# The first layer from its fourth tile on by quadrants with seven products for eight, its left sides streamed from DRAM

## Chip, cores and metric

One core of one Trainium2 chip. The metric is the time of one execution of the program on the device in microseconds (us); lower is better. Times are medians of several runs; stages are read from one execution recorded by the hardware profiler.

## What is computed

An attention with pooled keys and values (pooled by 8), and two dense layers of 512 to 2048 to 512 behind it, all in float32:

```python
scores = scale * np.matmul(q, k_p.transpose(0, 1, 3, 2))       # batch 8, 8 heads, 576 positions, 72 pooled keys
attn = np.exp(scores - np.max(scores, axis=-1, keepdims=True))
attn = attn / (np.sum(attn, axis=-1, keepdims=True) + 1e-09)
x = np.matmul(attn, v_p)                                       # to 4608 tokens x 512
h = x @ moe_w_in;  x = np.maximum(0.01 * h, h) @ moe_w_out     # first layer
h = x @ moe2_w_in; x = (h * np.clip(h + 3.0, 0.0, 6.0) / 6.0) @ moe2_w_out   # second layer
```

## The kernel before

Matrix products run in TensorE's float32r form. To keep the precision of float32 each operand is split in two parts, high and low, and each product is three matmuls: high x high, high x low, low x high.

**First layer.** The 4608 tokens are nine tiles of 512: tile b holds 512 of the 576 positions of batch b, and the ninth the 64 positions that are left of each of the eight batches. `moe_tile` takes one tile through 16 steps, one for each 128 columns of the hidden layer: `gemm1` (12 matmuls, lines 663 to 665), the leaky activation on ScalarE (line 678), the split of the result in `split_g` (a copy on ScalarE, line 286, and a subtraction on VectorE, line 296), and `gemm2` (12 matmuls, lines 712 to 714), which adds up in four banks of PSUM, y0 to y3. So a tile is 384 matmuls with 512 columns each. The sixteen weights w0 to w15 stay in SBUF, split, for all tiles; `decode_w` makes them from packed input words in the first two tiles. Tiles 0 and 1 are begun while batch 0 and 1 come out of the attention, in halves of 288 and 224 columns; tile 0 has a second part (weights 9 to 15) after tile 1.

**Attention.** Each batch is four units (`attend`): scores on TensorE, maxima on VectorE, exponentials on ScalarE (line 476), normalising on VectorE (line 508), transposes (lines 526, 544) and the product with the values (line 571) on TensorE. The units of batch t+1 are put among the steps of tile t, at `Jobs` slots (a tile has 34, one before each gemm1 and each gemm2).

**Second layer.** It goes by pairs of token groups (`Pair`), five pairs of 2 x 460 or 2 x 462 columns. The 2 x 2 quadrants of the weights and of the tokens are combined so that seven block products do for eight, in both products (`first` and `second`). A pair is 672 matmuls (line 911). The combined right sides are made by VectorE (`sides`, `second_sides`, line 818) and split; the combined left sides are made by `quadrant_weights` during tiles 2 to 8, stored to DRAM as w1s and w2s, and streamed back for every pair in transfers of 1 MB into four buffers (`stream`: raw twice, xh, xl).

**What sets the order.** All work is recorded as tasks, with an engine, a cost and the buffers that they read and write. `Plan.order` lays them out by repeated list scheduling with the costs and due times, forward and back, and the program is written in that order; each engine then works in its order. A buffer's tag with `bufs=n` rotates over n places in the order of the recording. All DMAs are issued by SyncE in one queue (SP), which waits at its head for what the next DMA needs. Where TensorE would wait in the beginning, `order` puts in fillers (`idle<-zeros`) up to `plan.fill_until`, the third step of tile 0.

Of the kernel before, what the change touches and what calls it, by code (L numbers as in the profile page):

```python
# [22 lines left out]
NF = DFF // 128  # L23
# [22 lines left out]
    slow=[0, 5, 5, 5, 5],  # L46
)
# [184 lines left out]
def attention_moe_moe(ctx: ExitStack, tc: tile.TileContext, qt, kt, vm, vr, wt, wq, eye, mask, out):  # L232
# [7 lines left out]

    nc = tc.nc
# [11 lines left out]
    def f32(ap):  # L253
        return ap.bitcast(F32)
# [58 lines left out]
    class Unit:  # L313


        def __init__(self, b, g, h):
            self.b, self.g, self.h = b, g, h
            self.fresh = h == 0
            self.early = b == 0 and h == 0
            self.whole32 = None  # L320
# [115 lines left out]
    def scores(u):  # L436

        assert held_keys[u.g] == u.b
        s = buf("s", [128, 1024], F32, 2)
# [114 lines left out]
    def values(u, x, spill):  # L554
# [19 lines left out]
        for pi, ps in enumerate(pss):  # L574
            k = 2 * u.g + pi

            if u.h == 0:
                dst = x((0, k), lambda t, k=k: t[:, k, 0:HALF])
                copy(dst, ps(None, lambda t: t[:, 0:HALF]), HALF, True, 0.125)
            else:  # L580
                n = TOK - HALF
                dst = x((1, k), lambda t, k=k: t[:, k, HALF:TOK])
# [5 lines left out]
    w = {}  # L588

# [5 lines left out]
    def decode(raw, t, l):  # L595

        words = lambda: raw.get().bitcast(I32).rearrange("p (n two) -> p n two", two=2)
        bits = lambda v: v.ap().bitcast(I32)

        on_act(1024, lambda: ACT.mul(out=t.ap(), in_=f32(words()[:, :, 1]), mul=2.0**-112), [raw()], [t])  # L600

        on_act(
            1024, lambda: ACT.mul(out=bits(l), in_=words()[:, :, 0].bitcast(U32), mul=7.49 / 2**32), [raw()], [l]
        )
        on_dve(
            1024,
# [7 lines left out]
            1024,  # L614
# [7 lines left out]
    def decode_w(f, raw, t, l):  # L622
# [7 lines left out]
        subtract(lo, t, hi, 1024)  # L630

# [11 lines left out]
    def split_x(x32, x, half=None):  # L643
        c0, c1 = (0, TOK) if half is None else HALVES[half]
        for k in range(4):
            cut = lambda t, k=k: four(t)[:, k, c0:c1]
            key = None if half is None else (half, k)
# [5 lines left out]
    def gemm1(f, x, c0, c1):  # L653
# [14 lines left out]
        keys = [(h, k) for h in part for k in range(4)]  # L668
# [89 lines left out]

    x2 = [buf(f"x2_{t}", [128, 4, TOK], pool=dram) for t in range(NT)]
    xr = buf("xr", [128, 4, B * REST], pool=dram)  # L760

    def store_y(ys, dst, r, last=False, plus=False):

        for o in range(4):
            v = r(("y", o), lambda t, o=o: four(t)[:, o, :])
# [11 lines left out]
            if o % 2 or last:  # L777
# [4 lines left out]
                    lambda o0=o0, o=o, d=d: DMA.dma_start(out=d(), in_=four(r.get())[:, o0 : o + 1, :]),  # L782
# [31 lines left out]
    w1s = [buf(f"w1s{j}", [128, PRODUCTS, 2, 512], F32R, pool=dram) for j in range(NF // 4)]  # L814
    w2s = [[buf(f"w2s{s}{h}", [128, 4, 512], F32R, pool=dram) for h in range(2)] for s in range(PRODUCTS)]
# [13 lines left out]
    def quadrant_weights(f):  # L829


        t = []
        for i in range(2):
# [7 lines left out]
            t.append(buf("s", [128, 1024], F32, 2))  # L841
            decode(raw, t[i](), buf("st", [128, 1024], F32, 3)())
        q = [[t[i](j, lambda t, j=j: t[:, 512 * j : 512 * j + 512]) for j in range(2)] for i in range(2)]

        def split_off(v, s):
            st = new_st(F32R)
            src = View(v.buf, v.key, lambda t: v.cut(t).rearrange("p (g n) -> p g n", g=2))
            hi, lo = [st(i, lambda t, i=i: t[:, :, 256 * i : 256 * i + 256]) for i in range(2)]
            copy(hi, src, 512)
            subtract(lo, src, hi, 512)  # L850
            for g, (dst, cut) in enumerate(
                [
                    (w1s[f // 2], lambda t: t[:, s, f % 2, :]),
                    (w2s[s][f // 4], lambda t: t[:, f % 4, :]),
                ]
            ):
                dst = dst((s, f), cut)
                on_dma(
                    262144,
                    lambda dst=dst, g=g: DMA.dma_start(out=f32(dst.ap()), in_=f32(st.get()[:, g, :])),  # L860
                    [st()],
                    [dst],
                )

        (q11, q12), (q21, q22) = q
        split_off(q11, 0)
        split_off(q12, 1)
        split_off(q22, 5)
        plus(q22, q21, q22, 512)
        split_off(q22, 4)  # L870
        minus(q21, q11, q21, 512)
        split_off(q21, 3)
# [549 lines left out]
```

## Time and profile before

| | |
|---|---|
| median of 3 runs | 1652.26 us (1652.09 to 1656.89) |
| the profiled execution: own time, span in the profile | 1655.2 us, 1652.9 us |
| matmuls of the built program, fillers among them | 7939, 201 |
| TensorE busy | 1639.3 us, 99% of the span |
| VectorE busy | 980.3 us, 59% |
| ScalarE busy | 894.7 us, 54% |
| DMA | 276.24 MB, 167 GB/s in the mean |

The profiled execution's own time is 2.94 us above the median of the runs. A matmul's recorded duration (390 ns) is longer than the distance between two of them, since they are pipelined; what a stage costs TensorE is read from how many there are in a stretch. The same holds for VectorE and ScalarE: of two instructions back to back, the distance between their starts counts.

### The profile page before, as it was taken

What the parts mean: (1) busy time and instruction counts of PE and PEld (TensorE: products, weight loads), DVE (VectorE), ACT (ScalarE), POOL (GpSimd) and SP (SyncE); (2) the same over time, 40 slices, a digit from 0 to 9 for tenths busy, and PEclk for the clock granted to TensorE, in tenths of its full rate; (3) what the DMA queues carried; (4) which work ended last, traced back from release to release, by engine and by line L of the source; (5) the groups of instructions that cost most, each with busy time, mean ns of one, the idle gap of its engine ahead of it and who ended that gap; (6) DMA issues with size and microseconds to landing.
All of it is one profiled execution on the core that took longest, in us unless ns stands there. A gap on an engine that the chain in (4) does not pass through costs nothing.

```text
span 1652.9 us, 22384 instructions
## 1 busy us (share of the span) xinstructions
PE 1639.3 (99%) x8169; PEld 1413.1 (85%) x8169; DVE 980.3 (59%) x1748; ACT 894.7 (54%) x2233; POOL 2.8 (0%) x14
## 2 busy tenths in 40 slices
PE   8999999999999999999999999999999999999999
PEld 8888888888888888888888898888889888888988
DVE  7996245545355454457421458846856875695584
ACT  7985355455554655556432345545555554564454
POOL 0000000000000000000000000000000000000000
PEclk9999999999999999999999999999999999999999
DMA  7642043323233231346610266776676586567564
GB/s 261 237 171 88 8 141 123 118 98 115 86 109 121 95 135 69 117 148 220 204 49 1 99 236 220 247 252 218 230 268 215 205 286 224 212 244 238 204 224 153
DMA packets 76925, 276.24 MB, mean 167 GB/s; under 512 B 13712, under 2 KB 26128, under 8 KB 55568
## 3 DMA queue, kind: packets, MB, share of 16 engines
q1 hardware_dynamic: 76816, 274.82, 47.7%
q8 instruction: 64, 1.05, 0.3%
q14 instruction: 45, 0.37, 0.1%
HBM read 223.41 MB, written 51.38 MB: 166 GB/s over the span
## 4 chain that ended last, share of the span: by engine, by line
PE 91%; DVE 5%; ACT 2%; DMA 1%; issue 1%; SPq 0%; DVEq 0%; ACTq 0%
PE y L911 17%; PE a L911 12%; PE h L911 11%; PE y L712 8%; PE y L713 8%; PE y L714 7%; PE h L663 7%; PE h L664 7%; PE h L665 7%; PE a L451 2%; PE a L571 2%; ACT s L476 1%; PE a L526 1%; DVE raw L354 1%; DMA raw<-kt 1%
## 5 line engine op out<-in xcount | busy, mean ns | idle before, releaser
L712 PE MATMUL y<-gh,w 128*128 128x512 f32 (+2 forms) x604 | 237.9, 394 | 0.0
L296 DVE TENSOR_TENSOR gl<-u,gh 128x512 fp32r<-128x512 f32 (+2 forms) x151 | 100.1, 663 | 231.7 <-ACT gh L286 231.4
L663 PE MATMUL h<-xh,w 128*128 128x512 f32 (+2 forms) x604 | 235.3, 390 | 1.3 <-ACT u L678 1.3
L713 PE MATMUL y<-gl,w 128*128 128x512 f32 (+2 forms) x604 | 232.5, 385 | 0.0
L714 PE MATMUL y<-gh,w 128*128 128x512 f32 (+2 forms) x604 | 231.6, 383 | 0.0
L664 PE MATMUL h<-xl,w 128*128 128x512 f32 (+2 forms) x604 | 230.7, 382 | 0.0
L665 PE MATMUL h<-xh,w 128*128 128x512 f32 (+2 forms) x604 | 230.6, 382 | 0.0
L678 ACT ACTIVATE u<-h 128x512 f32<-128x512 f32 (+2 forms) x151 | 87.9, 582 | 148.3 <-PE h L665 136.7
L286 ACT CAST gh<-u 128x512 fp32r<-128x512 f32 (+2 forms) x147 | 89.3, 608 | 133.6 <-PE y L714 108.3
L476 ACT ACTIVATE s<-a,mx 96x72 f32<-96x72 f32 x384 | 115.8, 325 | 39.4 <-DVE mx L470 39.4
L714 PEld LDWEIGHTS y<-gh,w 128*128 128x128 f32 x604 | 113.6, 188 | 24.6
L665 PEld LDWEIGHTS h<-xh,w 128*128 128x128 f32 x604 | 113.5, 188 | 23.5
L663 PEld LDWEIGHTS h<-xh,w 128*128 128x128 f32 x604 | 113.5, 188 | 23.4 <-ACT u L678 1.5
L664 PEld LDWEIGHTS h<-xl,w 128*128 128x128 f32 x604 | 113.6, 188 | 21.7
L712 PEld LDWEIGHTS y<-gh,w 128*128 128x128 f32 x604 | 113.7, 188 | 21.1
L713 PEld LDWEIGHTS y<-gl,w 128*128 128x128 f32 x604 | 113.8, 188 | 20.8 <-DVE gl L296 0.3
L289 ACT ACTIVATE gh<-w 128x460 fp32r<-128x460 f32 (+1 forms) x140 | 81.9, 588 | 66.9 <-PE y L911 37.3
L289 ACT ACTIVATE s<-w 128x460 fp32r<-128x460 f32 (+1 forms) x140 | 82.4, 589 | 64.8 <-PE y L911 33.5
L1089 DVE SCALAR_TENSOR_TENSOR s<-w,s 128x460 fp32r<-128x460 f32 (+1 forms) x140 | 88.7, 633 | 29.6 <-ACT s L289 29.5
L1089 DVE SCALAR_TENSOR_TENSOR gl<-w,gh 128x460 fp32r<-128x460 f32 (+1 forms) x140 | 88.2, 633 | 24.5 <-ACT gh L289 24.4
L911 PE MATMUL y<-w,raw 128*128 128x460 f32 (+1 forms) x384 | 86.3, 369 | 0.0
L476 ACT ACTIVATION_READ_ACCUMULATOR s<-a,mx 96x1 f32 x384 | 81.5, 212 | 0.0
(209 smaller groups left out, 3046.9 us busy)
## 6 DMA issues: line engine op xcount, KB each, us to landing
raw<-w2s SPq DMA_DIRECT2D x36, 1024.0 KB, 4.8
raw<-w1s SPq DMA_DIRECT2D x32, 1024.0 KB, 5.0
xh<-w1s SPq DMA_DIRECT2D x20, 1024.0 KB, 4.9
xh<-w2s SPq DMA_DIRECT2D x17, 1024.0 KB, 4.8
xl<-w2s SPq DMA_DIRECT2D x17, 1024.0 KB, 4.8
raw<-wq SPq DMA_DIRECT2D x16, 1024.0 KB, 5.0
w<-wt SPq DMA_DIRECT2D x15, 1024.0 KB, 7.3
w1s<-st SPq DMA_DIRECT2D x56, 256.0 KB, 2.2
```

What stands on the lines that cost most here:

```text
L286: a = lambda: ACT.copy(out=dst.ap(), in_=src.ap())
L289: a = lambda: ACT.mul(out=dst.ap(), in_=src.ap(), mul=scale)
L296: lambda: DVE.tensor_tensor(out=dst.ap(), in0=a.ap(), in1=f32(b.ap()), op=ALU.subtract),
L476: ACT.activation(out=at()[:, c, h, :], in_=s4()[:, c, e, :], func=AF.Exp, scale=1.0 / 64.0, bias=mx.get()[:, c, h : h + 1], accum_out=sm.g ...
L663: PE.matmul(out=o, lhsT=hi, rhs=xh.get()[:, k, c0:c1], start=k == 0, stop=False)
L664: PE.matmul(out=o, lhsT=hi, rhs=xl.get()[:, k, c0:c1], start=False, stop=False)
L665: PE.matmul(out=o, lhsT=lo, rhs=xh.get()[:, k, c0:c1], start=False, stop=k == 3)
L712: PE.matmul(out=y[:, n0:n1], lhsT=hi, rhs=gh.get()[:, n0:n1], start=start, stop=False)
L713: PE.matmul(out=y[:, c0:c1], lhsT=hi, rhs=gl.get()[:, c0:c1], start=False, stop=False)
L714: PE.matmul(out=y[:, c0:c1], lhsT=lo, rhs=gh.get()[:, c0:c1], start=False, stop=stop)
L911: PE.matmul(out=o, lhsT=l, rhs=r, start=first and i == m == 0, stop=last and i == len(left) - 1 and m == 2, skip_group_check=True,)
L1089: lambda: DVE.scalar_tensor_tensor(out=lo.ap(), in0=v.ap(), scalar=1.0 / 6.0, in1=f32(hi.ap()), op0=ALU.mult, op1=ALU.subtract),
```

## The change

Tiles 0, 1 and 2 stay as they were. The first layer's tiles 3 to 8 become three pairs of tiles, (3, 4), (5, 6) and (8, 7), each worked like a pair of the second layer, with 2 x 512 columns (`Pair1`, a subclass of `Pair`). What comes with it:

- Left sides of the first layer. `keep` (called by `decode_w`) stores each decoded weight to DRAM (chunk, 0.5 MB) and stores three quadrants of 0.25 MB of its split form directly (left1). `first_weights` reads chunks back, and makes the other four combinations (`combine`, `split_off`: 4 differences or sums, 4 copies, 4 subtractions), at slots of tiles 1, 0 (second part) and 2.
- Left sides of the second layer. `second_weights` does what `quadrant_weights` did, in halves of 512 columns: f = 0 and 1 in tile 1, f = 2 in the first pair, 3 and 4 in the second, 5 to 7 in the third.
- Streams of the new pairs come in pieces of 0.5 MB into six places, the halves of xh, xl and w15 (`rows = 2`).
- Attention. Batches 3 and 4 are done in tile 2 (eight units, three slots apart), 5 and 6 in the first pair, 7 in the second. A batch that must wait for its pair goes to DRAM (x1) and back.
- The exponentials' buffers are s and sb, one place each, in place of s with two. The results of tile 2 leave by st.

The diff, cut to its core:

```diff
@@ decode_w
     copy(hi, t, 1024)
     subtract(lo, t, hi, 1024)
+    keep(f, t, wf)
+
+def keep(f, t, wf):
+    d = chunk[f]()
+    on_dma(1 << 19, lambda: DMA.dma_start(out=d.ap(), in_=t.ap()), [t], [d])
+    r, lower = f % 8, f >= 8
+    for g, sides in enumerate(([(5, 1)], [(1, 0), (5, 1)]) if lower else ([(0, 0), (1, 1)], [(0, 0)])):
+        for s, h in sides:
...
...
+                    lambda dst=dst, g=g, h=h: DMA.dma_start(
...
+                        in_=f32(wf.get()[:, g : 4 : 2, 256 * h : 256 * h + 256]),
@@ left sides
+def combine(left, f, q):
+    (q11, q12), (q21, q22) = q
+    plus(q22, q21, q22, 512)
+    split_off(left, f, q22, 4)
+    minus(q21, q11, q21, 512)
+    split_off(left, f, q21, 3)
+    minus(q11, q22, q11, 512)
+    split_off(left, f, q11, 2)
+    minus(q12, q12, q11, 512)
+    split_off(left, f, q12, 6)
+def first_weights(f):
+    t = new_raw()
...
+    combine(left1[0], f, quarters(t))
+def second_weights(f):
...
+        for j in range(2):
+            decode(raw, q[i][j], new_st()(None, lambda t: t[:, 0, :]), j)
...
+    combine(left2, f, q)
@@ Pair.side (the right sides), for both layers
+        def side(self, s, b, split):
+            (b11, b12), (b21, b22) = b
+            if s == 2:
+                t2 = self.tmp()
+                minus(b11, b12, b11, n)
+                minus(t2, b22, b11, n)
+                minus(b21, b21, t2, n)
+                split(t2)
+            else:
+                if s == 3:
+                    minus(b12, b22, b12, n)
+                split({0: b11, 1: b21, 3: b12, 4: b11, 5: b21, 6: b22}[s])
@@ Pair1
+    class Pair1(Pair):
+        left = left1[0]
+        banks = {
+            "x": [("h", 2), ("h", 2), ("y0", 1), ("y1", 1)],
+            "z": [("y2", 1), ("y3", 1)],
+            "w": [("y0", 1), ("y1", 1), ("h", 2), ("h", 2)],
+        }
+        rows = 2
+        split_in = ["g", "sb", "g"]
+        def new_spare(self):
+            t, u = new_st(), buf("u", [128, 512])
+            self.spare = [u(), *(t(i, lambda t, i=i: t[:, i, :]) for i in range(2))]
+        def stream_to(self):
+            if not self.pieces:
+                for tag in ("xh", "xl", "w15"):
+                    t = buf(tag, [128, 4, 512], F32R)
+                    self.pieces.extend(t(i, lambda t, i=i: t[:, 2 * i : 2 * i + 2]) for i in range(2))
+            return lambda n: take("piece", self.pieces)
+        def activate(self, dst, h, in_psum):
+            leaky(dst, h, self.n, in_psum)
+        def place_of(self, i, j):
+            to = x2[self.tiles[j]]
@@ the main program
-    for t in range(2, NT):
-        jobs = Jobs()
...
-            attend_all(jobs, range(4 * t + 4, 4 * t + 8), (0, 8, 16, 24), held, SLOW)
-            jobs.at(14, lambda t=t: quadrant_weights(t - 2))
...
-        ys = moe_tile(x, jobs, FULL)
+    pairs1 = [Pair1(3, 4), Pair1(5, 6), Pair1(8, 7)]
+    jobs = Jobs()
+    attend_batch(jobs, 3, C["att3"][:4], C["gaps3"], True, chain=True)
+    held = attend_batch(jobs, 4, C["att3"][4:], C["gaps3"], False)
+    more_weights(jobs, first_weights, C["left1"][2])
+    prepare_pair(jobs, pairs1[0], x1[3], held, C["prep3"])
+    ys = moe_tile(x, jobs, FULL)
+    store_y(ys, to_dram(x2[2]), None)
+    jobs = pairs1[0].jobs
+    attend_batch(jobs, 5, C["att5"][:4], C["gaps5"], True, 0, True)
+    held = attend_batch(jobs, 6, C["att5"][4:], C["gaps5"], False)
+    prepare_pair(jobs, pairs1[1], x1[5], held, C["prep5"])
+    jobs = pairs1[1].jobs
+    held = attend_batch(jobs, 7, C["att7"], C["gaps7"], False, 0)
+    prepare_pair(jobs, pairs1[2], xr, held, C["prep7"])
+    for p, places in zip(pairs1, C["left2"]):
+        more_weights(p.jobs, second_weights, places)
```

**Place 1: SP's queue in the beginning.** The DMAs from the fourth weight of tile 0 on (`w<-wt` loads a packed weight, `raw<-kt`, `-vm`, `-vr` and `q<-qt` load the attention's inputs). Before:

```order
L592 DMA w_2_410<-wt 128x2048
L302 DMA raw_434<-kt 128x1152
L302 DMA q_447<-qt 128x576
L592 DMA w_2_517<-wt 128x2048
L302 DMA raw_570<-vr 96x512
L302 DMA raw_570<-vm 128x1024
L592 DMA w_3_722<-wt 128x2048
```

And with the change:

```order
L608 DMA w_2_410<-wt 128x2048
L651 DMA chunk_1_436<-w_1_76 128x1024
L315 DMA raw_449<-kt 128x1152
L651 DMA chunk_1_529<-w_1_374 128x1024
L608 DMA w_2_548<-wt 128x2048
L315 DMA q_585<-qt 128x576
L315 DMA raw_593<-vm 128x1024
L651 DMA chunk_1_648<-w_1_76 128x1024
L315 DMA raw_593<-vr 96x512
L663 DMA left_10_1_691<-w_1_412 128x2x256
L608 DMA w_3_704<-wt 128x2048
```

Between the first and the last of these weight loads now stand three stores of decoded weights and one of a split weight; each store waits at the queue's head for VectorE's last step on that weight.

**Place 2: VectorE in the third product of `second`.** Before, in the first pair of the second layer (L818 is a difference of two quadrants, w15 its spare buffer; L1089 a split's low part, gl or s; L296 belongs to the next pair's preparation):

```order
L1089 SCALAR_TENSOR_TENSOR gl_176_9290<-w15_10_8703,gh_176_9280 128x460
L296 TENSOR_TENSOR w6_3_9120<-x32_21_8587,w6_3_9120 128x460
L1089 SCALAR_TENSOR_TENSOR s_57_9292<-w15_10_8703,s_57_9292 128x460
L818 TENSOR_TENSOR w15_10_8703<-w11_3_8841 128x460
L1089 SCALAR_TENSOR_TENSOR gl_177_9308<-w15_10_8703,gh_177_9302 128x460
L818 TENSOR_TENSOR w15_10_8703<-w12_3_8854 128x460
L818 TENSOR_TENSOR w15_10_8703<-w13_3_8980 128x460
L1089 SCALAR_TENSOR_TENSOR s_58_9313<-w15_10_8703,s_58_9313 128x460
```

And with the change, in the first of the new pairs (L873 is the difference, u and st_71 the spares, L309 the split's low part, L479, L484 and the ones on sm and inv are the attention's last unit):

```order
L873 TENSOR_TENSOR u_56_4696<-w10_3_4519 128x512
L873 TENSOR_TENSOR st_71_5309<-w11_3_4988 128x512
L479 TENSOR_REDUCE mx_28_5811<-a_190_5803 96x3x2
L873 TENSOR_TENSOR w10_3_4519<-w10_3_4519,u_56_4696 128x512
L484 TENSOR_SCALAR mx_28_5811<-mx_28_5811 96x3x2
L309 TENSOR_TENSOR gl_68_5824<-st_71_5309,gh_68_5817 128x512
L479 TENSOR_REDUCE mx_28_5811<-a_191_5813 96x3x2
L873 TENSOR_TENSOR w11_3_4988<-w11_3_4988,st_71_5309 128x512
L484 TENSOR_SCALAR mx_28_5811<-mx_28_5811 96x3x2
```

The same stretch of differences and splits now has an attention unit's maxima between its instructions, and one spare buffer less.

## Rows read from the trace of the kernel before

**Rows 1.** The page: busy us (share of the span) and instructions

```profile
PE 1639.3 (99%) x8169; PEld 1413.1 (85%) x8169; DVE 980.3 (59%) x1748; ACT 894.7 (54%) x2233; POOL 2.8 (0%) x14
```

**Rows 2.** Waits of PE from 20 us on: us in total, times, longest

```profile
PE h L911 <- DVE gl L1089: 1.6, 4, 0.4
PE a L544 <- DVE tl L296: 1.5, 2, 1.4
```

**Rows 3.** Stretches: us, busy us by engine (instructions), PEclk, DMA share, GB/s

```profile
50.00:100.00 50.00, 47.99 (x280) 41.41 (x279) 48.42 (x81) 41.17 (x108) 0.29 (x1) 1.00 0.66 230
100.00:150.00 50.00, 48.32 (x315) 43.44 (x314) 44.69 (x93) 40.48 (x130) 0.00 (x0) 1.00 0.38 132
150.00:200.00 50.00, 50.00 (x237) 41.34 (x236) 12.65 (x22) 15.88 (x46) 0.00 (x0) 1.00 0.08 28
800.00:900.00 100.00, 100.00 (x434) 81.18 (x434) 26.19 (x40) 31.03 (x53) 0.00 (x0) 1.00 0.17 60
484.60:586.75 102.15, 102.15 (x502) 84.92 (x501) 50.37 (x95) 56.25 (x187) 0.00 (x0) 1.00 0.30 106
942.00:1083.00 141.00, 140.60 (x675) 126.28 (x674) 100.26 (x174) 75.28 (x133) 0.00 (x0) 1.00 0.69 241
1400.00:1500.00 100.00, 99.59 (x477) 89.19 (x477) 79.26 (x141) 57.36 (x102) 0.00 (x0) 1.00 0.67 232
```

**Rows 4.** The chain that ended last: the same scores of two tiles running

```profile
484.60 1.47 PE a L451 x12
586.75 1.47 PE a L451 x12
```

**Rows 5.** VectorE in time, tile 2: start us, us, instruction

```profile
308.05 0.68 DVE L296 TENSOR_TENSOR gl<-u,gh 128x512 fp32r<-128x512 f32 x1
308.65 0.68 DVE L296 TENSOR_TENSOR st<-s,st 128x512 fp32r<-128x512 f32 x1
315.59 0.95 DVE L508 TENSOR_TENSOR s<-s,inv 96x768 f32<-96x768 f32 x1
```

**Rows 6.** ScalarE in time, tile 2

```profile
306.19 0.62 ACT L286 CAST gh<-u 128x512 fp32r<-128x512 f32 x1
306.71 0.61 ACT L286 CAST st<-s 128x512 fp32r<-128x512 f32 x1
```

**Rows 7.** TensorE in time: the scores, fillers, and two waits of the beginning

```profile
305.67 1.63 PE L451 MATMUL a<-kbd,q 128*96 128x144 f32 x12
28.65 3.35 PE L1363 MATMUL idle<-zeros 128*128 128x128 bf16 x57
68.50 0.44 PE L526 MATMUL a<-ident,s 96*128 96x96 f32 x3 [0.44 <-DVE s L508]
71.91 0.42 PE L544 MATMUL a<-ident,rem 96*96 96x96 f32 x3 [1.35 <-DVE tl L296]
```

**Rows 8.** DMA issues: count, KB each, median us from issue to landing

```profile
raw<-w1s SPq DMA_DIRECT2D x32, 1024.0 KB, 5.0
xl<-w1s SPq DMA_DIRECT2D x12, 512.0 KB, 3.6
```

**Rows 9.** Two stretches of 10 us in the beginning, columns as in rows 3

```profile
10.00:20.00 10.00, 8.97 (x82) 8.38 (x82) 5.42 (x18) 7.76 (x47) 0.00 (x0) 1.00 1.03 377
120.00:130.00 10.00, 8.66 (x61) 7.97 (x60) 9.75 (x23) 6.67 (x34) 0.00 (x0) 1.00 0.83 302
```

**Rows 10.** Waits of SP's queue: us in total, times, longest

```profile
SPq L860 <- DVE st L296: 68.2, 34, 4.9
```

**Rows 11.** Groups with shapes apart: busy us, mean ns of decoding steps with 1024 columns

```profile
L607 DVE SCALAR_TENSOR_TENSOR st<-s,st 128x1024 int32<-128x1024 int32 x16 | 19.6, 1226 | 8.8 <-ACT s L600 6.2 <-ACT st L603 2.6
L600 ACT ACTIVATE s<-raw 128x1024 f32<-128x1024 f32 x16 | 18.4, 1150 | 1.6 <-DVE st L296 0.9 <-DMA raw<-wq 0.6
```

**Rows 12.** SP's queue in time: tile 0's partial result leaves, tile 1's leaves

```profile
103.71 1.52 SPq L782 DMA_DIRECT2D yp<-x  x2
208.36 0.33 SPq L782 DMA_DIRECT2D x<-raw  x1
```

**Rows 13.** The stretch between them, columns as in rows 3

```profile
104.00:208.00 104.00, 102.32 (x578) 88.32 (x577) 57.48 (x113) 58.24 (x180) 0.00 (x0) 1.00 0.21 73
```

More of the change, by code (lines that the diff above doesn't have):

```diff
@@ L1320, in attention_moe_moe, with attend_batch, start, end @@
     store_y(ys, to_dram(x2[0]), raw, plus=True)
+    def attend_batch(jobs, b, slots, gaps, store, begin=None, chain=False):
+        held = {}
+        units_of = units[4 * b : 4 * b + 4]
+        def start():
+            held.update(x=new_x32(), spill=new_spill())
+        def end():
+            store_rest(b, held["spill"])
+            if store:
+                on_dma(1 << 20, lambda: DMA.dma_start(out=x1[b].get(), in_=held["x"].get()), [held["x"]()], [x1[b]()])
+        def prepare_first():
+            u = units_of[0]
+            place(u)
+            fetch(u)
+            prepare(u)
+        if begin is not None:
+            jobs.at(begin, prepare_first)
+        jobs.at(slots[0] + gaps[3], start)
+        for n, (u, slot) in enumerate(zip(units_of, slots), 1):
+            nxt = units_of[n] if n < 4 else units[4 * b + 4] if chain else None
+            attend(jobs, u, slot, held, nxt, gaps)
+        jobs.at(slots[-1] + gaps[3], end)
+        return held
@@ new lines, in bring, with prepare_pair @@
+    def bring(src):
+        t = new_raw()
+        reload(t, src)
+        return t
+    def prepare_pair(jobs, p, src, held, slots):
+        a = {}
+        jobs.at(slots[0], lambda: a.update(a=bring(src)))
+        for k in range(2):
+            some = lambda k, which: p.prepare_some(k, p.quadrants(k, a["a"], held["x"]), which)
+            jobs.at(slots[0], lambda k=k: some(k, (0, 1)))
+            jobs.at(slots[1], lambda k=k: some(k, range(2, PRODUCTS)))
+    pairs1 = [Pair1(3, 4), Pair1(5, 6), Pair1(8, 7)]
@@ L1348, in attention_moe_moe @@
-    spare = buf("w15", [128, 4, 512])
-    for i, p in enumerate(pairs):
-        p.spare = spare
-        p.first()
-        nxt = pairs[i + 1] if i + 1 < len(pairs) else None
-        def between(s, f, nxt=nxt):
-            if nxt is not None and (s, f) in ((3, 0), (5, 0)):
-                nxt.spare = spare
-                nxt.prepare(int(s == 5))
-        p.second(nxt is None, between)
+    jobs = Jobs()
+    attend_batch(jobs, 3, C["att3"][:4], C["gaps3"], True, chain=True)
+    held = attend_batch(jobs, 4, C["att3"][4:], C["gaps3"], False)
```

376 lines of the change are left out of this document (202 added, 174 removed).

## The prediction

> **What bounds the kernel now.** First the page: TensorE is busy 99% of the span, VectorE 59%, ScalarE 54% [rows 1]. Then TensorE's waits: behind the first 20 us no kind of them comes to more than 1.6 us [rows 2]. The table of stretches shows the same by stage: from 150 us on TensorE has no idle time in the first layer, and loses 0.4 us in a pair of the second (140.60 of 141.00) [rows 3]. So the time is the number of matmuls times their distance. A stretch without attention holds 434 matmuls of 512 columns in 100 us, 0.2304 us each, at the full granted clock [rows 3]. Only between 50 and 150 us does TensorE idle, 2.0 + 1.7 us, and there VectorE is nearly full (48.42 of 50 us in the first half) [rows 3]; just behind, from 150 to 200 us, it is busy for 12.65 of 50.
>
> **What is removed.** A pair of tiles has 2 x 384 = 768 matmuls, a new pair 672, with the same 512 columns. Three pairs save 288; the built programs agree (7939 before, 7669 with the change, of which 18 more are fillers). 288 x 0.2304 = **66.4 us**, all of it on the path, since the stages concerned have no idle TensorE. The matmuls of attention and of the second layer stay as many.
>
> **What the new stages ask of the other engines.** Durations are distances of starts: 0.60 us for 512 columns on VectorE [rows 5], 0.52 on ScalarE [rows 6]. An attention unit: a tile with four units takes 586.75 - 484.60 = 102.15 us [rows 4], 384 matmuls of it 88.5, so a unit is 3.4 us of TensorE. Of that tile's 50.4 us of VectorE [rows 3], 22 instructions of 0.60 are the tile's own, and 4 x 1.23 [rows 11] + 11 x 0.60 make one weight's left sides; the remaining 25.7 us are 6.4 us a unit. Of its 56.25 us of ScalarE, 38 x 0.52 and 4 x 1.15 + 7 x 0.52 go off likewise; 28.2 remain, 7.1 us a unit.
>
> A new pair has on VectorE 22 instructions of preparing the next pair, 24 sums in the first product, 88 in the second (56 low parts and 32 differences) and 6 sums of results: 140 x 0.60 = 84 us. ScalarE has 14 + 56 + 56 + 8 = 134 x 0.52 = 69.7 us. One weight of `second_weights` is 19 x 0.60 = 11.4 and 15 x 0.52 = 7.8 us, one of `first_weights` 8 x 0.60 = 4.8 and 4 x 0.52 = 2.1 us. By stage, with TensorE in front:
>
> - Tile 2, with eight units, three first weights and the preparation: 88.5 + 27.2 = 115.7 us; VectorE 13.2 + 51.2 + 14.4 + 13.2 = 92.0 (80%); ScalarE 19.8 + 56.8 + 6.2 + 7.3 = 90.1 (78%).
> - First pair, eight units and one second weight: 154.8 + 27.2 = 182.0; VectorE 84 + 51.2 + 11.4 = 146.6 (81%); ScalarE 134.3 (74%).
> - Second pair, four units and two weights: 168.4; VectorE 132.4 (79%). Third pair, no units and three weights: 154.8; VectorE 118.2 (76%).
>
> The nearest row is a stretch of the second layer with VectorE at 79%, where TensorE lost 0.41 us in 100 [rows 3]. So the added work lies beside the matmuls, on average. I price four places where the average hides a shortage:
>
> 1. *The beginning.* 18 more fillers, 3.35 / 57 = 0.059 us each [rows 7], stand for **1.1 us** of planned waiting. `keep` puts 21 MB of stores on SP's queue, between weight loads that TensorE needs (place 1), while VectorE is full. Up to the store of tile 0's partial result the queue now moves 32.5 MB, 24.4 before, by the sizes in its order; that store came at 104 us [rows 12], so 312 GB/s are asked for, and the traffic there reached 302 and 377 GB/s at shares of 0.83 and 1.03 [rows 9]. TensorE idles 3.7 us in those 100 us now; I add as much again, **3 us** beside the fillers. Bounds: 0, if the stores find room, and 10, nearly three times today's loss. A gain is not excluded, as every order in there is new, but nothing takes work away.
> 2. *Tile 1.* Two weights of each kind fall in it: 32.4 us of VectorE, into 57.5 that stand there from 104 to 208 us [rows 12, 13], so 90 of 104. The room is at its end, where VectorE is idle now [rows 3]. I take **0**; where that cover is gone (the reload of tile 0's x must wait for the raw buffers these weights use), up to 5.
> 3. *Tile 2.* In the order, 33 to 36 matmuls now stand between a unit's scores and its transposes (60 before): 1.5 + 36 x 0.23 = 9.8 us. In the trace the scores start at 305.67 and are normalised at 315.59 + 0.95 = 316.54, 10.9 us later [rows 5, 7], with some 3 us of other work of VectorE in between. It can just be met, if units go first. In the beginning, with as little room, one unit waited 0.44 + 1.35 us [rows 7] and others not at all. I take 0.3 us for each of eight units, **2.4 us**; bounds 0 and 8 x 1.8 = 14.
> 4. *Second product of the first pair.* Its products 0 to 3 need 32 low parts and 32 differences, 38.4 us, and about two and a half units beside it, 16 us, so with two sums 55.6 us of VectorE against 44.2 + 8.5 = 52.7 of TensorE; place 2 shows the interleaving, with three spare buffers where there were four. **3 us** there, and 0.4 in each pair as in the second layer, **1.2 us** [rows 3]. Bounds 0 and 10.
>
> **Streams.** A new pair reads 56 pieces of 0.5 MB, one for 12 matmuls, 2.77 us. 0.5 MB took 3.6 us to land, 1 MB 5.0 [rows 8]. Six places make a piece due 13.8 us after the place came free, so 10 us are spare; the longest wait of SP for a store's data was 4.9 us [rows 10]. By the sizes in SP's order the three pairs move 49.4, 46.7 and 49.7 MB, 271, 277 and 321 GB/s against the 241 of a pair of the second layer [rows 3] and 377 at the most [rows 9]. I take 0. The Trainium skill, page "DMA: Bandwidth & Descriptors", section "Bandwidth", speaks against pieces this small: it asks for transfers of 1 MiB or more for 75% of the peak, and its fit (2.0 us and 436 GB/s) gives 3.2 us for half a MB, an estimate; one after the other they would make the first layer's pairs 179 us instead of 154.8. The trace has 3.6 us, close, but 241 GB/s of mostly 1 MB pieces that take 5.0 us each, more than one at a time allows (210 GB/s): they overlap, and by that the rule does not price the stream.
>
> **Sum.** Against the profiled execution: 1655.2 - 66.4 + 1.1 + 3 + 2.4 + 4.2 = 1599.5 us. Its time is 2.9 us above the median of the runs shown, so **1597 us**. With nothing lost anywhere it is 1586; with the four places at their upper ends (1.1 + 10 + 5 + 14 + 10 + 1.2 us) it is 1627. I take values near the lower ends, since the nearest rows, today's beginning and the second layer, run at these loads with small losses.
>
> **Rivals.**
>
> *A: no room for latency (1605 to 1640, at 1622).* VectorE and ScalarE work in fixed orders, and a unit's chain crosses them six times. If each of the 16 units in tile 2 and the first pair loses the 1.8 us of the slow unit [rows 7], that is 29 us in place of 2.4, and the time is 1597 + 26 = 1623. For it: three slots instead of five, 80% average load, place 2. Against it: the planner puts a waiting unit first, and most units of the beginning did not wait.
>
> *B: the streams bind, slower than before.* SP's queue is one, and its head waits. If pieces come one at a time, because each stands behind a store or a load that waits, a pair takes 56 x 3.6 = 202 us: 20, 33 and 47 us more than TensorE's 182, 168 and 155, 100 us in all, and 1597 + 100 = 1697. It decides for "slower" once a piece comes every 3.2 us instead of 2.77 (66 us over 168 pieces is 0.39 each, against pairs that attention stretches). Against it: pieces overlap today [rows 3, 9], and each has ten us of spare time. By the fit of the Trainium skill, page "DMA: Bandwidth & Descriptors", a piece would take 3.2 us, an estimate, just this border.
>
> *C: the matmuls leave, but another engine sets the pairs' length.* VectorE would need 40% more than its rows give: 205, 185 and 165 us against 182, 168 and 155, 51 us in all, and 1648, within 0.3% of before. No stretch seen speaks for that much [rows 3].
>
> **How the numbers follow.** My forecast, with losses between 0 and some 18 us (1586 to 1604), 0.66; A 0.24; B 0.05; C 0.02; a beginning that comes out faster, below 1586, 0.03. A measurement of this kernel tells about 0.3% (5 us) from no change. Forecast, A and the last are faster, 0.93; C is the same, 0.02; B slower, 0.05. The range reaches from 1586, all places at their lower ends, to 1616, which takes in about half of A; left out are the other half, B, C and the 0.03 below, some 0.2.
>
> **What would show it.** Right: matmuls fall by 270 with fillers, TensorE stays at 98 to 99% of a span near 1597; in the three pairs the stretches hold 672 matmuls and show VectorE near 80%; DMA rises to about 413 MB. Step 1 is read from TensorE's idle time between 50 and 150 us (near 7 us instead of 3.7), step 3 from waits of the transposes (lines 540 and 558) for VectorE in tile 2, step 4 from waits of line 974 for the low parts in the first pair. Wrong: line 974 waiting for DMAs into xh, xl or w15 (B), TensorE's waits for VectorE or ScalarE above 20 us in tile 2 and the first pair (A), or TensorE busy below 96%.

## The result, and the profile after

The changed kernel takes **1625.6 us** in the median of its four runs (1622.4 to 1627.8), the kernel before beside it 1652.9 us: a ratio of 0.983, 95% interval 0.981 to 0.985. It is faster by 27 us where 66.4 us of matmuls left and 55 were forecast; the range (1586 to 1616) missed it by 10 us. It is faster by more than the spread of the runs, and by half of what was forecast. The profiled execution took 1624.8 us, its span is 1623.0 us.

The page of the changed kernel: busy us of the engines, DMA in sum, and the chain that ended last.

```profile
PE 1588.9 (98%) x7899; PEld 1361.6 (84%) x7899; DVE 1188.2 (73%) x2122; ACT 1009.3 (62%) x2481; POOL 2.8 (0%) x14
...
DMA packets 134981, 414.73 MB, mean 256 GB/s; under 512 B 19024, under 2 KB 51920, under 8 KB 113104
...
PE 66%; DVE 11%; DMA 9%; ACT 4%; issue 2%; SPq 1%; ACTq 0%; DVEq 0%
```

270 matmuls are gone, as the edit says [rows 1], yet TensorE is busy only 50.4 us less and idle 34.1 us of its span, against 13.6 before. DMA holds 9% of the chain, against 1% before. The stretches of the changed kernel, columns as in [rows 3]:

```profile
50.00:100.00 50.00, 46.80 (x267) 40.04 (x266) 45.85 (x83) 39.36 (x118) 0.00 (x0) 0.97 0.89 306
100.00:150.00 50.00, 47.47 (x300) 42.49 (x299) 47.43 (x95) 42.38 (x130) 0.28 (x1) 0.97 0.93 312
200.00:250.00 50.00, 47.35 (x236) 38.43 (x234) 33.62 (x61) 32.48 (x100) 0.00 (x0) 1.00 0.92 308
250.00:300.00 50.00, 47.06 (x227) 38.98 (x228) 38.73 (x74) 30.05 (x101) 0.00 (x0) 0.97 0.89 298
400.00:500.00 100.00, 96.24 (x491) 78.84 (x489) 77.33 (x157) 79.50 (x281) 0.00 (x0) 1.00 0.86 285
500.00:600.00 100.00, 96.84 (x453) 78.51 (x452) 89.14 (x160) 68.89 (x183) 0.00 (x0) 1.00 0.74 243
```

TensorE now idles 2.5 to 3.2 us in each of these stretches of 50 us (between 150 and 200 us it does not), and in the first pair (386 to 586 us) 3 to 4 in each hundred. VectorE is not full between 200 and 300 us (34 to 39 of 50), so it is not the amount of its work that TensorE waits for there. In the first pair it comes nearer to that: 77 of 100 us, then 89. What differs most from before is the DMA share: 0.89 and 0.93 between 50 and 150 us, where [rows 3] has 0.66 and 0.38. PEclk, the granted clock, is 0.97 in three of the rows.

Where the time went, stage by stage: for every matmul the distance to the next start less the usual one of its shape (0.2304 us for 512 columns, as in the prediction; fillers count whole), summed. That is 38.8 us over the kernel before and 75.4 over the changed one, 36.6 more, and 66.4 - 36.6 = 29.8 is what the two spans differ by (29.9); lost time is defined so that this must come out, so it checks the counting and not a cause. The prices are the prediction's, with its 0.4 us for each pair.

| stage of the changed kernel | lost beyond the same work before, us | priced |
|---|---|---|
| up to 105 us (beginning, fillers) | 2.4 | 4.1 |
| tile 1, 105 to 217 us | 4.1 | 0 |
| tile 0's second part, 217 to 267 us | 5.4 | no term |
| tile 2, 267 to 386 us | 3.6 | 2.4 |
| first pair, first product, to 491 us | 10.1 | 0.4 |
| first pair, second product, to 586 us | 4.6 | 3.0 |
| second and third pair | 3.9 | 0.8 |
| second layer | 2.5 | 0 |

The longest waits of the changed kernel for DMAs (us in total, times, longest), ScalarE's for x<-x (15.0 us, most of it in the second layer) left out, and the only one of a new pair's matmuls:

```profile
ACT st L299 <- DMA left<-st: 23.9, 20, 3.7
ACT raw L617 <- DMA raw<-wq: 12.3, 9, 2.4
DVE raw L873 <- DMA raw<-chunk: 9.3, 7, 3.6
DVE raw L368 <- DMA raw<-vr: 7.5, 3, 4.5
DVE raw L368 <- DMA raw<-kt: 7.5, 6, 2.7
DVE raw L368 <- DMA raw<-vm: 6.4, 5, 2.7
PE y L974 <- DMA xh<-left: 2.2, 1, 2.2
```

ScalarE and VectorE stand 67 us in these rows in front of DMAs that have not landed. All waits of these two engines for DMAs come to 99 us, against 49 in the kernel before. Such a wait costs time only where TensorE's work stands behind it: before, VectorE stood 20 us for raw<-kt and raw<-vr between 150 and 900 us, and TensorE idled for 0.1 us there. How a wait reaches TensorE is seen at the largest stall. VectorE of the changed kernel in time (start us, us, instruction, idle time ahead and who ended it), and TensorE:

```profile
247.44 0.69 DVE L873 TENSOR_TENSOR raw<-raw 128x512 f32<-128x512 f32 x1 [1.95 <-DMA raw<-chunk]
249.38 2.14 DVE L873 TENSOR_TENSOR raw<-raw 128x512 f32<-128x512 f32 x3 [1.25 <-DMA raw<-chunk]
251.45 0.81 DVE L309 TENSOR_TENSOR tl<-a,th 128x288 fp32r<-128x288 f32 x2
```

```profile
247.87 0.39 PE L753 MATMUL y<-gh,w 128*128 128x512 f32 x1
251.95 0.71 PE L558 MATMUL a<-ident,rem 96*96 96x96 f32 x3 [3.70 <-DVE tl L309]
...
252.94 0.63 PE L752 MATMUL y<-gl,w 128*128 128x512 f32 x1
```

VectorE stands at the sums of a first weight, 1.95 and 1.25 us, for a load of the copies. Behind them in its order stand the low parts of a unit's transposed scores (tl), for which TensorE waits 3.70 us; then its matmuls show 0.63 us in place of 0.39, and the granted clock between 252 and 255 us is 0.50, the lower level. This is in tile 0's second part. In the second product of the first pair it is the same picture with other names: pooling of values (line 368) stands in front of a low part (sb) that a piece's matmuls need.

```profile
560.87 0.68 DVE L368 TENSOR_REDUCE raw<-raw 96x64 f32<-96x512 f32 x1 [2.47 <-DMA raw<-vr]
561.47 0.68 DVE L309 TENSOR_TENSOR sb<-w,sb 128x512 fp32r<-128x512 f32 x1
```

And in the first product of the first pair, where most is lost, the chain that ended last goes from a load of values over its pooling to the normalising of scores (line 522), for which TensorE waits 1.47 us at 449 us:

```profile
439.85 6.04 DMA raw<-vm
...
445.91 0.07 DVE raw L368
...
447.90 0.87 DVE s L522
```

Another 2.2 us there are a wait of the matmuls themselves for a piece of the stream (xh<-left, 6.2 us from issue to landing), and some 1.5 the lowered clock behind it.

Why the orders are made so that work stands behind a load: DMA issues of the kernel before (count, KB each, median us from issue to landing), and of the changed one.

```profile
w1s<-st SPq DMA_DIRECT2D x56, 256.0 KB, 2.2
raw<-vm SPq DMA_DIRECT2D x15, 512.0 KB, 3.5
raw<-vr SPq DMA_DIRECT2D x15, 192.0 KB, 2.6
```

```profile
left<-st SPq DMA_DIRECT2D x176, 256.0 KB, 4.6
raw<-chunk SPq DMA_DIRECT2D x32, 256.0 KB, 4.5
raw<-vm SPq DMA_DIRECT2D x15, 512.0 KB, 5.3
raw<-vr SPq DMA_DIRECT2D x15, 192.0 KB, 5.0
```

The planner (`Plan.lag` and `on_dma`) reckons bytes/350 + 50 ns for a transfer and 900 ns from its end to the first use: 0.80 + 0.9 = 1.7 us for 256 KB, 2.4 us for 512 KB. Before, landings took 0.5 to 1.1 us more than that; now they take 2.8 to 2.9 us more, and for the 192 KB of raw<-vr 3.5. So an engine told to do the sums "when the load is in" is told so some 3 us early, and everything behind waits. The 3 us are an estimate: the plan lays transfers one behind another, so a part of them may stand in it as queueing.

The Trainium skill, page "DMA: Bandwidth & Descriptors", section "Anatomy of one DMA — SWDGE (gpsimd) path", has 2.0 us and the bytes at 436 GB/s, which makes an estimate of 2.6 us for 256 KB. This is the fit that the prediction takes; it is for DMAs that GpSimd issues, and here SyncE issues them. The trace before is near it (2.2); with the DMA engines at 0.9 the load of 256 KB took 4.5 us, and this decides. The same page of the Trainium skill, section "Latency and other measured facts", says that the fixed part shrinks with lighter HBM load; the two traces agree in direction.

Two theories stand against each other. **L**: VectorE and ScalarE work in fixed orders made with landings that are too early, and what stands behind a late landing reaches TensorE. **C**: rival A of the prediction, a unit's chain is too long for its slots. Variants of L differ in the cure: order alone (L1), or a structure that has no better order (L2).

### The profile page after: what moved, and what is told of

Read it like the earlier page. It is cut to its first block, busy times and chain, and to the rows that moved or that the text cites. A ratio compares the mean times of both kernels' runs of the same rounds, so it can differ in the third digit from the quotient of the medians.

```text
span 1623.0 us, 23182 instructions
## 1 busy us (share of the span) xinstructions
PE 1588.9 (98%) x7899; PEld 1361.6 (84%) x7899; DVE 1188.2 (73%) x2122; ACT 1009.3 (62%) x2481; POOL 2.8 (0%) x14
## 4 chain that ended last, share of the span: by engine, by line
PE 66%; DVE 11%; DMA 9%; ACT 4%; issue 2%; SPq 1%; ACTq 0%; DVEq 0%
PE y L974 29%; PE h L974 18%; PE a L974 12%; DMA left<-st 3%; DVE w L873 2%; DMA raw<-chunk 1%; DMA raw<-vm 1%; PE a L465 1%; DVE gl L309 1%; PE a L585 1%; DMA x<-x 1%; DVE st L309 1%; PE y L751 1%; PE y L752 1%; PE y L753 1%
## 5 line engine op out<-in xcount | busy, mean ns | idle before, releaser
L873 DVE TENSOR_TENSOR w<-y,w 128x512 f32<-128x512 f32 (+2 forms) x108 | 70.3, 657 | 73.7 <-PE y L974 73.6
L974 PE MATMUL y<-w,xh 128*128 128x512 f32 (+2 forms) x444 | 106.0, 386 | 2.6 <-DMA xh<-left 2.2
L873 DVE TENSOR_TENSOR w<-w 128x460 f32<-128x460 f32 (+2 forms) x168 | 106.0, 648 | 2.1 <-ACT w L717 1.2
L974 PEld LDWEIGHTS y<-w,xh 128*128 128x128 f32 x444 | 83.7, 190 | 16.6 <-DMA xh<-left 2.5
L751 PE MATMUL y<-gh,w 128*128 128x512 f32 (+2 forms) x220 | 85.0, 386 | 0.0
L702 PE MATMUL h<-xh,w 128*128 128x512 f32 (+2 forms) x220 | 83.6, 380 | 0.0
L752 PE MATMUL y<-gl,w 128*128 128x512 f32 (+2 forms) x220 | 81.3, 369 | 2.0 <-DVE gl L309 1.9
L704 PE MATMUL h<-xh,w 128*128 128x512 f32 (+2 forms) x220 | 81.8, 372 | 0.0
L703 PE MATMUL h<-xl,w 128*128 128x512 f32 (+2 forms) x220 | 81.6, 371 | 0.0
L753 PE MATMUL y<-gh,w 128*128 128x512 f32 (+2 forms) x220 | 81.0, 368 | 0.0
L974 PE MATMUL y<-w,xl 128*128 128x512 f32 (+2 forms) x324 | 79.0, 386 | 0.0
L974 PEld LDWEIGHTS y<-w,raw 128*128 128x128 f32 x384 | 71.9, 188 | 8.1 <-DVE w L873 0.5
L309 DVE TENSOR_TENSOR st<-raw,st 128x512 fp32r<-128x512 f32 x88 | 60.0, 686 | 21.3 <-ACT st L299 20.8
L309 DVE TENSOR_TENSOR gl<-w,gh 128x512 fp32r<-128x512 f32 x96 | 65.6, 685 | 10.5 <-ACT gh L299 10.1
L873 DVE TENSOR_TENSOR w<-h,w 128x512 f32<-128x512 f32 (+2 forms) x44 | 29.0, 663 | 59.1 <-PE h L974 59.0
```

Of the source, the lines that this page charges most:

```text
L309: lambda: DVE.tensor_tensor(out=dst.ap(), in0=a.ap(), in1=f32(b.ap()), op=ALU.subtract),
L702: PE.matmul(out=o, lhsT=hi, rhs=xh.get()[:, k, c0:c1], start=k == 0, stop=False)
L703: PE.matmul(out=o, lhsT=hi, rhs=xl.get()[:, k, c0:c1], start=False, stop=False)
L704: PE.matmul(out=o, lhsT=lo, rhs=xh.get()[:, k, c0:c1], start=False, stop=k == 3)
L751: PE.matmul(out=y[:, n0:n1], lhsT=hi, rhs=gh.get()[:, n0:n1], start=start, stop=False)
L752: PE.matmul(out=y[:, c0:c1], lhsT=hi, rhs=gl.get()[:, c0:c1], start=False, stop=False)
```

## The experiments

Each was timed beside the kernel before on the same chip (runs 1 to 3, 4 and 5, and 6 to 8 on three chips; the kernel before took 1654.0, 1654.5 and 1653.8 us there). In the texts on the runs, tile 0' is the second part of tile 0, and the planner's own end is the time that the planner itself reckons for its order. The lost time is summed as above, by stretch, from the profiled executions (that of run 4 was 4 us faster than the median of its runs, that of run 1 3 us):

| us lost in | before | after | 2.5 us | 3.5 us | moved | moved, 3.0 us |
|---|---|---|---|---|---|---|
| 0 to 50 | 23.5 | 23.0 | 24.1 | 23.7 | 22.3 | 24.4 |
| 50 to 150 | 6.0 | 11.6 | 2.3 | 4.0 | 8.7 | 2.7 |
| 150 to 300 | 1.2 | 9.3 | 15.3 | 21.7 | 4.2 | 1.2 |
| 300 to 600 | 1.6 | 18.6 | 8.8 | 3.4 | 16.0 | 3.9 |
| 600 to 900 | 1.4 | 5.2 | 9.8 | 8.7 | 8.1 | 5.0 |
| 900 to the end | 5.2 | 7.8 | 6.9 | 6.9 | 7.7 | 6.7 |
| median of runs | 1652.9 | 1625.6 | 1616.1 | 1618.3 | 1620.2 | 1593.4 |

**1. Fewer bytes, same order.**

```
-        DMA.dma_start(out=d.ap(), in_=t.ap())
+        DMA.dma_start(out=d.ap()[0:m], in_=t.ap()[0:m])
```

and the same for the stores of left sides; m is 128 for weights 0 and 1 of a half, else 32, and the loads read what is whole.

> The order of every engine, the number of DMAs and every wait are those of the changed kernel; of the stores into the weights' copies and into the first layer's left sides, those of weights 2 to 7 of either half move 32 partitions of 128, about 21 MB less, nearly all in the first 300 us. What the pairs and the sums read in their place is what was stored whole for weights 0 and 1, so the left sides of the other weights are left out of the first layer's pairs. Theory L (the 26 us behind the priced losses come from landings: DMA engines at 0.9 of their time make a 256 KB load take 4.5 us, and VectorE, whose order is fixed, stands at line 873 or 368 for it with the attention's or the splits' work behind): loads of the copies land in about 3 us, VectorE's waits at line 873 fall from 9.3 to under 5 us, TensorE's stall of 3.9 us at 252 us shrinks, and the time falls by 6 to 14 us, to 1611 to 1619. Theory C (the chain of a unit is too long for its slots, the rival A of the prediction): within 4 us of the changed kernel's 1625.6, since no computation has moved. Theory S (SP's queue stands at its head for a store's data, whatever the size of the store): within 4 us as well, with SP's waits at line 900 as long as now (73 us).

Measured: 1614.3 us, ratio 0.977 (0.975 to 0.978), 11 us less than the changed kernel. A stretch, a wait and a load of this run:

```profile
200.00:250.00 50.00, 49.48 (x245) 40.50 (x243) 38.93 (x71) 33.96 (x108) 0.00 (x0) 1.00 0.64 200
```

```profile
DVE raw L877 <- DMA raw<-chunk: 4.7, 5, 1.6
```

```profile
raw<-chunk SPq DMA_DIRECT2D x32, 256.0 KB, 4.1
```

L holds in time and waits: VectorE's waits for the copies halve, the stall at 252 us goes, and no stretch before 900 us is at a lowered clock. It was wrong in the size of the landings, which fell to 4.1 us and not to 3; the thin stores themselves landed sooner (left<-w in 3.0 us, 4.8 in the changed kernel), and what each gave of the 11 us is not told apart. C and S fall as accounts of the whole, for nothing but bytes was changed: SP's waits at its line 900 stayed (73.9 us), as S expected, and yet the time fell. Most of the first pair's loss stays, so that C could still hold there; the next runs test it.

**2 and 3. The planner told of later landings.** `fill_until` ends the beginning; the other hunks only hand the task's number to `lag`. The second run has 3500.

```
+    LANDING = 2500
-    def lag(self, a, b):
+    def lag(self, a, b, i=0):
+        if a == "dma" and b != "dma" and i > self.fill_until:
+            return self.LANDING
```

> Only the order changes: behind the beginning the planner reckons with 2.5 us in place of 0.9 between the end of a transfer and its first use. Theory L with a cure by order (L1: VectorE stands behind landings because the planner believes them early): VectorE's waits for DMAs at lines 873 and 368 (9.3 + 21.4 us now) fall to about half, TensorE's stalls over 0.3 us in tile 0' to the first pair with them, and the time falls by 8 to 16 us, to 1610 to 1618. Rival L2 (the work has no other order: two places of raw serve the reloads, the first weights and attention's keys and values, so that whoever comes late costs TensorE): waits only change their engine, the time stays within 5 us of 1625.6; the planner's own end is 16 us later with this lag. Theory C: no change or slower, since units start later for the same slots.

> As the run before with 3.5 us in place of 0.9. L1: VectorE's waits at lines 873 and 368 fall to a third or less, time 1608 to 1618, near that of the run with 2.5. L2: slower than the run with 2.5 us by up to 9 us (the planner's own end is 25 us later than the changed kernel's, 9 later than with 2.5), at 1625 or above. Theory C: 1625 or slower.

Measured: 1616.1 us (0.977, 0.975 to 0.978) and 1618.3 us (0.979, 0.977 to 0.980). Both sides were half right. VectorE's waits for loads at these two lines fall from 30.7 us to 14.0 and 4.6, as L1 expected. With 3.5 us the stretch from 300 to 600 us loses 3.4 us in place of 18.6, with the same slots and the same work: C falls there, and L1 holds. But 150 to 300 us loses 12 us more than in the changed kernel, and 600 to 900 us 4 more in both runs, most of it by one stall near 845 us and the lowered clock beside it. Two stretches of the run with 3.5 us:

```profile
200.00:250.00 50.00, 39.80 (x171) 30.82 (x170) 28.41 (x46) 24.37 (x53) 0.00 (x0) 0.86 0.82 268
...
400.00:500.00 100.00, 99.51 (x518) 82.99 (x517) 82.39 (x167) 82.84 (x292) 0.00 (x0) 1.00 0.84 289
```

The chain that ended last of this run, up to TensorE's wait of 7.8 us at 217 us:

```profile
205.63 4.24 DMA left<-st
...
209.97 0.63 ACT st L303
...
210.62 0.70 DVE st L313
...
211.35 1.12 ACT raw L621
...
213.50 1.24 DVE raw L626
...
216.02 1.05 ACT w L303
...
217.12 0.79 PE h L706
```

The decoding of a weight that tile 1 itself needs (lines 621 to 634, then its cast) comes behind a left side's part (st), which had waited for its place: the store out of it took 4.24 us to land. At the end of tile 1 more left sides are made than the places of st and raw let through, once landings are reckoned as late. That is the part of L2 that was right; that it is the places is argued here from the chain, and the next two runs test it.

**4. One weight's left sides moved out of tile 1**, the planner as in the changed kernel.

```
-    left0=[(0, 13), (1, 20)],
+    left0=[(0, 13)],
-    left2=[[(2, 24)], [(3, 30), (4, 43)], [(5, 0), (6, 16), (7, 32)]],
+    left2=[[(2, 24)], [(3, 30), (4, 43), (1, 32)], [(5, 0), (6, 16), (7, 32)]],
```

> One piece of work moves: the left sides of the second layer's weight 1 are made in the second pair (slot 32) in place of the end of tile 1; the planner is that of the changed kernel (0.9 us behind a transfer). Its own end is 3 us earlier than the changed kernel's. Theory T (the transition from tile 1 to tile 0' is short of places: first weights, a second weight and the reload of x pass through two places of raw in the last 20 us of tile 1, and a late landing there costs TensorE): TensorE's losses between 200 and 300 us fall from 9.0 to under 4 us, the half-clock interval at 252 us goes, the later stalls stay since the order is still planned with early landings; time 1613 to 1621. Rival O (only the order is to blame, and a weight moved changes nothing without it): within 4 us of 1625.6.

Measured: 1620.2 us, 0.979 (0.977 to 0.982). By the time alone T and O are hardly told apart: 5 us less than the changed kernel, where O allows 4, and the runs of the two overlap (1616.2 to 1624.2, and 1622.4 to 1627.8). The stretches speak for T: the loss between 150 and 300 us falls from 9.3 to 4.2 us, TensorE idles 1.3 us in place of 2.65 between 200 and 250, and the lowered clock at 252 us goes. That from 300 to 600 stays, near enough (16.0 for 18.6); the other stretches move by up to 3 us either way, and a lowered clock comes up at 315 us.

```profile
200.00:250.00 50.00, 48.67 (x257) 40.86 (x256) 36.59 (x70) 32.93 (x109) 0.00 (x0) 1.00 0.86 279
```

**5. Both.**

> The same move, and the order planned with 3.0 us between the end of a transfer and its use in place of 0.9, behind the beginning. If T and L1 are both right, the losses of the runs with 2.5 and 3.5 us between 150 and 270 us (15 to 22 us) go, the pairs stay as free of stalls as there, and only the place near 840 us (8 us there; the planner now shows 2.8 us of it) and the half clock behind it remain: time 1595 to 1604. If T is wrong (the two places of raw are short whatever is moved): 1612 to 1620, as the runs with 2.5 and 3.5 us.

Measured: **1593.4 us** (1593.0 to 1594.1), 0.963 (0.962 to 0.965), faster than both kernels. The page, stretches, waits and landings of this run:

```profile
PE 1576.8 (99%) x7878; PEld 1356.8 (85%) x7878; DVE 1185.6 (74%) x2122; ACT 1007.2 (63%) x2481; POOL 2.8 (0%) x14
```

```profile
150.00:200.00 50.00, 50.00 (x247) 41.63 (x246) 28.44 (x46) 27.64 (x66) 0.00 (x0) 1.00 0.95 331
200.00:250.00 50.00, 50.00 (x251) 41.61 (x250) 36.87 (x69) 33.60 (x109) 0.00 (x0) 1.00 0.75 246
...
400.00:500.00 100.00, 99.59 (x515) 82.47 (x514) 83.97 (x167) 81.50 (x292) 0.00 (x0) 1.00 0.82 279
500.00:600.00 100.00, 99.59 (x460) 81.57 (x459) 80.50 (x145) 71.14 (x176) 0.00 (x0) 1.00 0.86 293
```

```profile
DVE raw L372 <- DMA raw<-vm: 4.0, 4, 1.8
ACT raw L621 <- DMA raw<-wq: 4.0, 3, 1.6
```

```profile
left<-st SPq DMA_DIRECT2D x176, 256.0 KB, 4.5
...
raw<-vm SPq DMA_DIRECT2D x15, 512.0 KB, 5.8
```

The landings are about as late as in the changed kernel (4.5 us for 4.6, 5.8 for 5.3; the copies 4.1 for 4.5) and the DMA engines at 0.95 from 150 to 200 us; VectorE and ScalarE have as many instructions (2122 and 2481), TensorE 21 fillers less. But hardly anything stands behind a landing any more: of ScalarE's 23.9 us for left<-st and VectorE's 9.3 for raw<-chunk nothing is left, all waits of the two for DMAs come to 27 us in place of 99, and TensorE is without idle time from 150 to 250 us. Apart, the two edits gave 5 and 7 to 10 us (with 3.5 and 2.5 us; 3.0 without the move was not run); together 32.

**6. Version 5 with the thin stores.** The diffs of 1 and 5.

> The version with the moved weight and the order planned with 3.0 us (1593.4 us), in the same order, with the thin stores of the first run: weights 2 to 7 of either half store 32 partitions of 128 into the copies and the first layer's left sides, which are left out of the computation as there; 21 MB less. Theory L1 (traffic costs only where the order does not reckon with the landings it makes): no more to be had, within 3 us of 1593.4, where the same cut gave 11 us on the changed kernel. Rival B1 (the DMA engines bind in the beginning in any order): another 5 to 11 us, 1582 to 1588.

Measured: 1593.0 us, 0.963 (0.962 to 0.965). A cut of 21 MB that gave 11 us on the changed kernel gives 0.4 here. B1 falls; the bytes cost here only through an order that did not reckon with them. The stretch that was at 0.95 is at 0.74:

```profile
150.00:200.00 50.00, 50.00 (x244) 41.47 (x243) 27.86 (x45) 27.58 (x65) 0.00 (x0) 1.00 0.74 237
```

**7. The later landings reckoned for VectorE alone.**

```
-        if a == "dma" and b != "dma" and i > self.fill_until:
+        if a == "dma" and b == "dve" and i > self.fill_until:
```

> As the version of 1593.4 us, but the 3.0 us are reckoned only from a transfer to VectorE; ScalarE and TensorE are planned with 0.9 us as in the changed kernel. If VectorE's place behind landings is the whole of it (L1 in its narrow form): 1592 to 1600. If ScalarE's waits for the left sides of the next pair's places of st and for raw, and TensorE's for pieces, count as much: 1602 to 1612.

Measured: 1604.7 us, 0.971 (0.969 to 0.972), the second case. ScalarE's waits are back, and 8.5 of the 11 us that this run loses beyond run 5 lie between 300 and 900 us. The two rows:

```profile
ACT st L303 <- DMA left<-st: 22.1, 23, 2.5
ACT raw L621 <- DMA raw<-wq: 11.4, 7, 2.4
```

So L in its narrow form, VectorE alone, was too narrow: of the gain of 27 us over the run with the moved weight only (1620.2), some 16 come from VectorE's place and 11 from the others' (ScalarE's and TensorE's were not tried apart).

**8. The kernel before with the same planner.**

> The kernel before, with its order planned with 3.0 us in place of 0.9. Where the DMA engines are idle half the time and nothing of the first layer behind 150 us waits, early landings in the plan cost nothing: L1 expects the same time within 4 us (its beginning loses some 6 us between 50 and 150 us, of which a part may come back). If reckoning with late landings were a gain of its own, apart from what the change brings: 8 us or more less, below 1645.

Measured: 1649.8 us, 0.997 (0.997 to 0.998): 4.0 us, on the border named, and its loss between 50 and 150 us falls from 6.0 to 3.0. The other rival falls: reckoning with late landings gives 4 us here and 27 in the changed kernel with the moved weight. What the planner was not told cost little until the change put 138 MB more on the DMA engines.

## Why the prediction was wrong

- **What is removed: right.** Under a planner that reckons with 3.0 us the change, with one weight's left sides moved, is worth 1649.8 - 1593.4 = 56.4 us, and the lost times of these two runs differ by 44.0 - 33.6 = 10.4 us: together 66.8, against 66.4.
- **The step that failed: "So the added work lies beside the matmuls, on average. I price four places where the average hides a shortage."** The four places came out at 2.4, 4.1, 3.6 and 4.6 us, 14.7 in all where 9.5 were priced, and each within its own bounds. What the sum put at nothing, or at 0.4 us for a pair, came to 21.9 us: 10.1 in the first product of the first pair, 5.4 in tile 0's second part, 3.9 in the second and third pair, 2.5 in the second layer. Of the 25.9 us that were not forecast, 20.7 lie there. In the first pair's first product and in tile 0's second part, 15.5 of the 21.9 us, the wait that it left out is that of VectorE and ScalarE for DMAs that land later than before, with TensorE's next work behind it in their fixed orders: in run 5, with later landings in the plan and one weight moved, the first pair's two products lose 1.2 and 1.1 us in all, and tile 0's second part 0.3. For the other pairs and the second layer that is not shown: run 5 loses there nearly as much as the changed kernel (5.0 us for 5.2 between 600 and 900 us, and 6.7 for 7.8 behind).
- **Term 1, the beginning: right** (2.4 us for 4.1; by its own sign, TensorE's idle time between 50 and 150 us, 5.7 us for 7). The first 50 us, where the fillers are, lose no more than before (23.0 us for 23.5).
- **Term 2, tile 1, "I take 0":** 4.1 us, within its bound of 5 but not nothing. It added up VectorE's busy time (90 of 104 us). VectorE had the room; what costs TensorE is the place of its work in the order. The 2.1 us at 145 us stand behind a store out of st that took 4.2 us to land, and behind it the clock is low.
- **Tile 0's second part has no term at all.** Three first weights are made there, and the largest stall of the kernel (3.7 us at 252 us) stands at their loads. With one second weight less in tile 1 all that it loses falls from 6.0 to 2.5 us (run 4).
- **Term 3, tile 2:** 3.6 us for 2.4. The two longest stalls there (1.2 and 1.7 us) stand behind a raw<-chunk of 6.9 us and a raw<-vr of 4.6.
- **Term 4, second product of the first pair:** 4.6 us for 3, within its bound, but not for its reason, VectorE's load (55.6 us of work in 52.7). Between 500 and 550 us VectorE is busy for 50.00 of 50 us and TensorE idles 0.2; the two long stalls come behind it, at loads for the pooling. With as many instructions of VectorE, run 5 loses 1.1 us.
- **Streams, "I take 0":** for the pieces this nearly held (one wait of 2.2 us, and the clock behind it). But the step only asked whether pieces come in time. The same traffic makes other landings late, and the 3.6 and 5.0 us of [rows 8] come from stretches at a share near 0.67 [rows 3], where the changed kernel is at 0.74 to 0.93.
- **"I take values near the lower ends, since the nearest rows, today's beginning and the second layer, run at these loads with small losses":** the loads of VectorE were the same, the DMA share was not. The prediction had worked out 312 GB/s for the beginning and up to 321 in the pairs, and did not ask what a landing takes then.
- **Against rival A stood "the planner puts a waiting unit first".** That holds only as far as the planner's landings hold. A's time (1623) was nearly met, but by luck: it charged 1.8 us to each of 16 units for want of slots. By the prediction's own sign for A, TensorE's waits for VectorE and ScalarE in tile 2 and the first pair, it is 10 us and not above 20, and with the same slots the run with 3.5 us loses 2.5 us in the first pair.
- **Rivals B and C:** refuted. Line 974 waits for a DMA once, 2.2 us, and with the DMA engines at 0.95 for 50 us run 5 has no such wait. VectorE is as busy there as in the changed kernel (1185.6 us, 1188.2).
- **Not priced at all: the clock.** Four times in the changed kernel matmuls ran at 1.2 in place of 2.4 GHz behind a stall of 2 to 4 us, some 6 us of the 36.6. In run 5 no stretch before 900 us shows it.

The range was not too low because of a bound: with the four places at their upper ends the sum gave 1627, which would have held the measured 1625.6, though the time went elsewhere. The range ended at 1616 by the choice to take in half of A.

Open: of the 10 us that the change still loses in run 5 against run 8, about 2 us lie in the first 50 us and 4 between 600 and 900. Of these, 1.7 are a stall at 823 us: VectorE is busy for 18.00 of the 18 us before it, and the chain there has no DMA, so there the load does bind. The rest was not taken apart. The moved weight was planned with 0.9 and 3.0 us alone; how much of the 32 us hangs on just this order, among others that values near it would give, is not known. A third place of raw was not tried.

## What to carry to other kernels

An order that is fixed ahead, by hand or by a planner, holds as long as the times it was made with. Here a change that added traffic moved the median landings of the attention's and the left sides' transfers from 2.2 to 3.5 us to 4.6 to 5.3. So compare the planner's time to first use with the medians of issue to landing at the DMA share that the change will make, before adding up busy times. If an engine has room on average and TensorE still waits, look at what its instruction stands behind, not at how much it does. And go through every stage, also those whose work seems covered: four fifths of the miss here lay in stages that the sum priced at nothing or nearly so. Two cures that give little each (5 and 7 to 10 us) were worth 32 together, as either left the other's place as the next wait.

## What was not expected of the hardware

At the DMA shares of the changed kernel's first 900 us (0.82 in the mean; 0.31 before, from 150 us on) the size of a transfer tells less of when it lands: 192 KB (raw<-vr) took 5.0 us and 512 KB (raw<-vm) 5.3, where before they took 2.6 and 3.5; 1 MB (raw<-wq) took 7.1, before 5.0. In the second layer, at a share near 0.65 with and without the change, 1 MB pieces took 4.8 to 5.0 in both kernels. A cut of the stores by 21 MB took the DMA share from 0.92 to 0.64 between 200 and 250 us, while the median landing of the copies only went from 4.5 to 4.1 us. In run 5 the DMA engines were at 0.95 of their time from 150 to 200 us, 331 GB/s, and TensorE had no idle time there. And the clock: it fell behind a stall of 2.1 to 3.9 us four times in the changed kernel and behind one of 2.0 us in run 4, but not behind one of 2.3 us in run 1 nor one of 1.9 us in run 5; in the run with 3.5 us, where TensorE stood still for 7.8 us, the row of 50 us shows a mean of 0.86. The length of a stall alone does not tell, in these runs, whether the clock falls.
